# Half of the ELU gates on GpSimd in two operations, and projections that close only the gates they read

## The chip, the cores and the metric

The kernel runs on one core of a Trainium2 chip. The metric is the device time of one execution in microseconds (us); lower is better. Times are medians of several runs of the same program, and beside them stands one execution that was taken with the hardware profiler. The engines are named as in the profile: PE is TensorE's matmul, PEld its weight load, DVE is VectorE, ACT is ScalarE, POOL is GpSimd, SP is SyncE.

## What is computed

A top-32 attention is followed by a two-layer feed-forward net with an ELU between the layers. There are 8 batches, 8 heads, 576 tokens and a head size of 64; the model width is 512 and the hidden width 2048.

```python
scores = scale * np.matmul(q, k.transpose(0, 1, 3, 2))
kth = np.partition(scores, -top_k, axis=-1)[..., -top_k:-top_k + 1]
scores = np.where(scores >= kth, scores, -1000000000.0)
attn = np.exp(scores - np.max(scores, axis=-1, keepdims=True))
attn = attn / (np.sum(attn, axis=-1, keepdims=True) + 1e-09)
x = np.matmul(attn, v)            # heads side by side: 4608 x 512
h = x @ w_in                      # 4608 x 2048
g = np.where(h > 0.0, h, np.exp(np.minimum(h, 0.0)) - 1.0)
out = g @ w_out                   # 4608 x 512
```

## The kernel before

The attention is cut into 144 steps. A step is one tile of 128 queries of one batch with two heads (for the left-over 64 queries of each batch, four heads). The loop at the end of the kernel runs over the steps and, in each, writes out the work of several of them: it computes the scores of the step two ahead (`scores`: matmuls L300, copies on ACT L308), selects the 32nd largest score of the current step (`select`: on DVE alone, eight MAX8, L341 and L353, and six MATCH_REPLACE8, L346, in each step), masks and exponentiates the step before (`mask`: two tiny POOL operations, `neg` L366 and `gap` L368, and then two ACT passes, L369 and L370, for each head), normalises it (`normalise`: five tiny POOL operations L380 to L385 and two wide ones L387), transposes the step before that (`turn`: PE L406, ACT copies L407), and multiplies by V (`attend`: PE L432, ACT L459).

When all heads of a block of tokens are there, the feed-forward net of the block is put into a queue of pieces (`ffn_pieces`). A block has one, two or three slots of 128 tokens. First come 16 pieces `hidden(f)`, one for each group f of 128 hidden units: four matmuls into one of two PSUM buffers (L490), then on ACT a ReLU of the negated values into a tile n (L502), a ReLU into gT (L503) and an exponential of n (L504). What is then missing of the ELU is called the gate: gT becomes (n - 1) + gT, one SCALAR_TENSOR_TENSOR on DVE (L471). After them come four pieces `project(s, part)` for each slot s: each multiplies four groups of gT by w_out (L513) and the last of them copies the sum out (L522).

The function `feed` is called four times in each step. It counts up `place`, closes the gates that were put into a list at least two feeds ago (L604), and takes as many pieces from the queue as a plan by costs and due steps gives (`HIDDEN`, `PROJECT`). A gate is therefore not written where its exponential is, but some two feeds, half a step, later. Two other places close gates: `hidden` closes the oldest when more than three are open (L485 to L487), and `project` closes all that are open (L508). At the end a loop writes out what is left in the queue, with no feeds between.

From step 8 on the order on PE, ACT, DVE and POOL is the order in which the program is written (`manual_schedule`); in the eight steps before a scheduler may move instructions. In those first steps the weights also arrive as 64-bit floats and are decoded to 32 bits, on ACT (L169 to L171), POOL (L172, L186) and DVE (L179, L182). The first five blocks have one slot, so their gates are 128 columns wide; later gates are 256 or 384 wide. In all there are 304 gates.

Of the kernel before, what the change touches and what calls it, by code (L numbers as in the profile page):

```python
# [9 lines left out]
ALU = mybir.AluOpType  # L10
# [70 lines left out]
def kernel(  # L81
# [9 lines left out]
    nc = tc.nc  # L91
# [9 lines left out]
    NF = dff // P  # L101
# [362 lines left out]
    gates = []  # L464
    place = [0]

    def close_gates(keep=0):

        while gates and gates[0][0] <= place[0] - keep:
            _, dst, n = gates.pop(0)  # L470
            nc.vector.scalar_tensor_tensor(  # L471
                out=dst, in0=n, scalar=-1.0, in1=dst, op0=ALU.add, op1=ALU.add
            )

    def ffn_pieces(blk):
        n_tok = blk.slots * P

        def hidden(f):
            if f == 0 and blk.number == 0:
                g = early.tile([P, NF, P], FP32, tag="g", name="gT")  # L480
                blk.gT = [g[:, 0:NG], g[:, NG:NF]]
            elif f % NG == 0 and blk.number > 0:
                g = late["g"].tile([P, NG, T], FP32, tag="g", name="gT")
                blk.gT.append(g[:])
            if len(gates) > 3:  # L485
                gates[0] = (-1, *gates[0][1:])
                close_gates(place[0])  # L487
            ps = ps_f.tile([P, dm], FP32, tag="f", name="hps")
            for i in range(NC):
                nc.tensor.matmul(  # L490
                    ps[:, 0:n_tok],
                    w_in[:, i, f * P : (f + 1) * P],
                    blk.xT[:, i, 0:n_tok],
                    start=(i == 0),
                    stop=(i == NC - 1),
                )
            if blk.number == 0:
                n = earlyf.tile([P, P], FP32, tag="n", name="n")[:]
            else:
                n = late["f"].tile([P, T], FP32, tag="n", name="n")[:, 0:n_tok]  # L500
            g = blk.gT[f // NG][:, f % NG, 0:n_tok]
            nc.scalar.activation(n, ps[:, 0:n_tok], AF.Relu, scale=-1.0)  # L502
            nc.scalar.activation(g, ps[:, 0:n_tok], AF.Relu)  # L503
            nc.scalar.activation(n, n, AF.Exp, scale=-1.0)  # L504
            gates.append((place[0], g, n))

        def project(s, part):
            close_gates()  # L508
            if part == 0:
                blk.o = ps_f.tile([P, dm], FP32, tag="f", name="ops")  # L510
            step = NF // 4
            for f in range(part * step, (part + 1) * step):
                nc.tensor.matmul(  # L513
                    blk.o[:],
                    blk.gT[f // NG][:, f % NG, s * P : (s + 1) * P],
                    w_out[:, f, :],
                    start=(f == 0),
                    stop=(f == NF - 1),
                )
            if part == 3:  # L520
                o = opool.tile([P, dm], FP32, tag="osb", name="osb")
                nc.scalar.copy(o[:], blk.o[:])  # L522
                for t in blk.tiles[s]:
                    p0 = t.cols.start - s * P
                    nc.sync.dma_start(out[t.rows, :], o[p0 : p0 + t.ql, :])

        part = HIDDEN[blk.slots]
        behind = 2 * NF if blk.number else 0
        return [
            (part, max(behind, NC * (f // 4 + 1)), lambda f=f: hidden(f))  # L530
            for f in range(NF)
        ] + [
            (PROJECT, max(behind, NF + (part + 1) * NF // 4),
             lambda s=s, part=part: project(s, part))
            for s in range(blk.slots)
            for part in range(4)
        ]
# [4 lines left out]
    for b in range(B):  # L542
        if b % 2 == 0:
# [5 lines left out]
            for part in division:  # L549
                blk = Block(len(blocks), len(part))  # L550
# [20 lines left out]
        for qts in order:  # L571
            for hp in range(NHP // 2 if qts == (J,) else NHP):
                group = Group([tiles[qt] for qt in qts], hp)
                steps += [Step(tiles[qt], hp, group, i) for i, qt in enumerate(qts)]
            for qt in qts:
                n = len(steps)
# [12 lines left out]
    for b in range(1, B):  # L589
        f = first[b]  # L590
# [10 lines left out]
    def feed(n, share):  # L601

        place[0] += 1
        close_gates(2)  # L604
        fed["at"] = max(fed["at"], n)
        ahead = [(w - fed["sum"]) / (x - fed["at"]) for x, w in due if x > fed["at"]]
        if ahead:
            fed["over"] += max(0.0, share * min(ahead))
        fed["at"] += share
        while ffn and decoded[0] >= ffn[0][1] and 0.5 * ffn[0][0] <= fed["over"]:  # L610
            cost, _, piece = ffn.pop(0)
            fed["over"] -= cost
            fed["sum"] += cost
            piece()
# [115 lines left out]
```

## Time and profile before

| What | us |
|---|---|
| median of three runs (1694.2 to 1695.28) | 1694.59 |
| the profiled execution, its own time | 1695.23 |
| span of the profile, first to last instruction | 1693.4 |
| PE busy, 8560 matmuls | 1597.5 (94%) |
| DVE busy, 3248 instructions | 1542.7 (91%) |
| ACT busy | 1179.6 (70%) |
| POOL busy | 627.0 (37%) |

The profile page gives the busy time of each engine over the span, a strip of 40 slices with the busy share of each in tenths, the chain of work that ended last, and groups of instructions by line and shape. A row of a group has its count, the busy time in us, the mean of one in ns, and the idle time of the engine just before these instructions with what ended it. The trace answers further questions: busy times in chosen stretches of time, of all instructions or of one line's alone; who waited for whom; and the instructions in order of time. The ends of matmuls are modelled and matmuls overlap, so a PE that is always busy need not run at its peak.

### The profile page before, as it was taken

What the parts mean: (1) busy time and instruction counts of PE and PEld (TensorE: products, weight loads), DVE (VectorE), ACT (ScalarE), POOL (GpSimd) and SP (SyncE); (2) the same over time, 40 slices, a digit from 0 to 9 for tenths busy, and PEclk for the clock granted to TensorE, in tenths of its full rate; (3) what the DMA queues carried; (4) which work ended last, traced back from release to release, by engine and by line L of the source; (5) the groups of instructions that cost most, each with busy time, mean ns of one, the idle gap of its engine ahead of it and who ended that gap; (6) DMA issues with size and microseconds to landing.
All of it is one profiled execution on the core that took longest, in us unless ns stands there. A gap on an engine that the chain in (4) does not pass through costs nothing.

```text
span 1693.4 us, 26805 instructions
## 1 busy us (share of the span) xinstructions
PE 1597.5 (94%) x8560; PEld 1035.0 (61%) x8560; DVE 1542.7 (91%) x3248; ACT 1179.6 (70%) x2813; POOL 627.0 (37%) x1719
## 2 busy tenths in 40 slices
PE   4568899999999999999999999999999999999999
PEld 3355676667575666756557575755557575755565
DVE  6889999999999999999999999999998999998600
ACT  5787776778776776857758585867758686857531
POOL 3675333343333333433333333333333333332200
PEclk8568999999999999999999999999999999999999
DMA  5531021001200111001100111001100000000000
GB/s 156 169 130 63 15 56 36 7 1 42 51 12 7 29 35 42 1 14 42 43 19 1 28 42 35 7 10 46 36 20 8 21 21 28 7 7 7 7 13 13
DMA packets 101131, 56.25 MB, mean 33 GB/s; under 512 B 84096, under 2 KB 92288, under 8 KB 100992
## 3 DMA queue, kind: packets, MB, share of 16 engines
q1 hardware_dynamic: 100992, 54.55, 11.7%
q8 instruction: 68, 1.11, 0.3%
q14 instruction: 71, 0.58, 0.1%
HBM read 45.09 MB, written 9.44 MB: 32 GB/s over the span
## 4 chain that ended last, share of the span: by engine, by line
PE 68%; DVE 21%; ACT 5%; issue 2%; POOL 2%; DMA 1%; SPq 0%; ACTq 0%; POOLq 0%; DVEq 0%
PE ops L513 25%; PE hps L490 21%; PE avps L432 8%; DVE wk L346 7%; PE scps L300 7%; DVE m L353 6%; PE eps L406 5%; DVE m L341 2%; DVE gT L471 1%; DVE wk L323 1%; DVE m L329 1%; PE qkps L270 1%; ACT sc L370 1%; ACT sc L369 1%; ACT et L407 1%
## 5 line engine op out<-in xcount | busy, mean ns | idle before, releaser
L353 DVE MAX8 m<-wk 128x8 f32<-128x576 f32 x816 | 574.9, 745 | 0.0
L490 PE MATMUL hps<-xT,w_in 128*128 128x256 f32 (+2 forms) x2432 | 554.3, 376 | 19.3 <-ACT gT L503 19.3
L513 PE MATMUL ops<-w_out,gT 128*128 128x512 f32 x1152 | 522.6, 598 | 0.0
L490 PEld LDWEIGHTS hps<-xT,w_in 128*128 128x128 f32 x2432 | 409.5, 194 | 119.9 <-ACT gT L503 26.4
L346 DVE MATCH_REPLACE8 wk<-m,wk 128x576 f32<-128x576 f32 x544 | 399.4, 741 | 0.0
L513 PEld LDWEIGHTS ops<-w_out,gT 128*128 128x128 f32 x1152 | 208.4, 190 | 232.8 <-issue 201.0
L380 POOL TENSOR_SCALAR dene<-den 128x2 f32<-128x2 f32 x144 | 34.9, 243 | 819.6 <-ACT sc L370 819.0
L369 ACT ACTIVATE sc<-sc,neg 128x576 f32<-128x576 f32 x288 | 226.5, 787 | 56.6 <-POOL neg L366 56.1
L370 ACT ACTIVATE sc<-sc,gap 128x576 f32<-128x576 f32 x288 | 223.2, 775 | 26.6 <-ACT sc L369 1.9
L308 ACT ACTIVATE sc<-scps 128x576 f32<-128x576 f32 x288 | 173.4, 661 | 82.4 <-PE scps L300 82.4
L387 POOL TENSOR_SCALAR sc<-sc,rec 128x576 f32<-128x576 f32 x288 | 218.7, 769 | 15.2 <-POOL rec L385 0.4
L300 PE MATMUL scps<-kqT 64*128 64x288 f32 (+1 forms) x1280 | 198.1, 438 | 21.5 <-ACT sc L308 14.7
L471 DVE SCALAR_TENSOR_TENSOR gT<-n,gT 128x256 f32<-128x256 f32 (+2 forms) x304 | 129.1, 431 | 95.3 <-ACT n L504 95.3
L407 ACT COPY et<-eps 128x512 f32<-128x512 f32 x288 | 167.4, 581 | 61.8 <-PE eps L406 61.8
L406 PEld LDWEIGHTS eps<-ident,sc 128*128 128x128 f32 x1152 | 144.5, 145 | 93.4 <-issue 48.9
L346 DVE MATCH_REPLACE8 wk<-m,sc 128x576 f32<-128x576 f32 x272 | 199.7, 741 | 0.0
L432 PE MATMUL avps<-et,vT 128*64 128x256 f32 (+2 forms) x2080 | 191.0, 325 | 9.0 <-ACT et L407 8.4
L406 PE MATMUL eps<-ident,sc 128*128 128x128 f32 x1152 | 177.9, 280 | 21.8 <-POOL sc L387 18.6
L341 DVE MAX8 m<-sc 128x8 f32<-128x576 f32 x272 | 191.3, 744 | 0.0
L432 PEld LDWEIGHTS avps<-et,vT 128*64 128x64 f32 x2080 | 122.3, 140 | 80.4 <-issue 24.7
L502 ACT ACTIVATE n<-hps 128x256 f32<-128x256 f32 (+2 forms) x304 | 112.6, 370 | 84.2 <-PE hps L490 79.0
L300 PEld LDWEIGHTS scps<-kqT 64*128 64x128 f32 (+1 forms) x1280 | 106.0, 180 | 90.2 <-issue 45.1
(47 smaller groups left out, 1236.6 us busy)
## 6 DMA issues: line engine op xcount, KB each, us to landing
kin<-in_k_dram SPq DMA_DIRECT2D x64, 128.0 KB, 2.8
qin<-in_q_dram SPq DMA_DIRECT2D x64, 128.0 KB, 2.8
raw<-in_moe_w_in_dram SPq DMA_DIRECT2D x16, 512.0 KB, 3.9
vT<-in_v_dram SPq DMA_DIRECT2D x64, 128.0 KB, 2.3
raw<-in_moe_w_out_dram SPq DMA_DIRECT2D x16, 512.0 KB, 3.3
out_dram<-osb SPq DMA_DIRECT2D x32, 256.0 KB, 2.2
kin<-in_k_dram SPq DMA_DIRECT2D x32, 32.0 KB, 2.5
kin<-in_q_dram SPq DMA_DIRECT2D x32, 32.0 KB, 2.2
```

The lines of the kernel that those rows point to most:

```text
L300: nc.tensor.matmul(wide[i][rows, half, 0:HS], kq[part, q0 : q0 + u.t.ql], kq[part, k0 : k0 + HS], start=True, stop=True,)
L341: nc.vector.max(found[i], cur[i])
L346: nc.vector.match_replace(wk[i], found[i], cur[i], TAKEN)
L353: nc.vector.max(found[i], cur[i])
L369: nc.scalar.activation(sc, sc, AF.Prelu, bias=neg[:], alpha=STEEP)
L370: nc.scalar.activation(sc, sc, AF.Exp, bias=gap[:], accum_out=u.den[:, i : i + 1])
L387: nc.gpsimd.tensor_scalar(u.sc[:, i, :], u.sc[:, i, :], rec[:, i : i + 1], 1.0, ALU.mult, ALU.mult)
L406: nc.tensor.transpose(ps[:, c * P : (c + 1) * P], sc[:, c0 : c0 + P], ident[:])
L407: nc.scalar.copy(g.et[:, chunks, u.at, :], ps[:, 0 : n * P].rearrange("p (c q) -> p c q", c=n),)
L432: nc.tensor.matmul(ps[i * D : (i + 1) * D, cols], vt[:, 2 * J + i if c == J else i * J + c, :], w, start=(c == 0), stop=(c == J),)
L490: nc.tensor.matmul(ps[:, 0:n_tok], w_in[:, i, f * P : (f + 1) * P], blk.xT[:, i, 0:n_tok], start=(i == 0), stop=(i == NC - 1),)
L513: nc.tensor.matmul(blk.o[:], blk.gT[f // NG][:, f % NG, s * P : (s + 1) * P], w_out[:, f, :], start=(f == 0), stop=(f == NF - 1),)
```

## The change

Each gate is stored with its block and group. A gate of an even group stays on DVE as it was. A gate of an odd group goes to POOL, in two operations: n - 1 into n, and gT + n into gT. A projection closes the gates of its own block up to the last group that it reads, no longer all that are open. The rule in `hidden` closes the oldest gate as before, written in the new way.

```diff
-    def close_gates(keep=0):
-
-        while gates and gates[0][0] <= place[0] - keep:
-            _, dst, n = gates.pop(0)
-            nc.vector.scalar_tensor_tensor(
-                out=dst, in0=n, scalar=-1.0, in1=dst, op0=ALU.add, op1=ALU.add
-            )
+    def close_gates(keep=0, upto=None):
...
+        while gates:
+            put, group, dst, n = gates[0]
+            if put > place[0] - keep if upto is None else group > upto:
+                return
+            gates.pop(0)
+            if group[1] % 2 == 0:
+                nc.vector.scalar_tensor_tensor(
+                    out=dst, in0=n, scalar=-1.0, in1=dst, op0=ALU.add, op1=ALU.add
+                )
+            else:
+                nc.gpsimd.tensor_scalar_add(n, n, -1.0)
+                nc.gpsimd.tensor_tensor(dst, dst, n, ALU.add)
...
             if len(gates) > 3:
-                gates[0] = (-1, *gates[0][1:])
-                close_gates(place[0])
+                close_gates(upto=gates[0][1])
...
-            gates.append((place[0], g, n))
+            gates.append((place[0], (blk.number, f), g, n))
 
         def project(s, part):
-            close_gates()
+            close_gates(upto=(blk.number, (part + 1) * NF // 4 - 1))
```

Set side by side, the two built programs have the same instructions in the same order on PE, ACT and SP. DVE has 152 gates fewer (2234 instructions for 2386, as the program counts them), and 15 others, in the first steps, stand at another place. POOL has 304 operations more (2028 for 1724), and 3 others, in the first steps too, stand at another place.

## The prediction on record

> **What bounds the kernel now.** I read the page's busy strip first, then the groups by line and shape, then the busy times in chosen stretches, then the waits.
>
> ```profile
> span 1693.4 us, 26805 instructions
> PE 1597.5 (94%) x8560; PEld 1035.0 (61%) x8560; DVE 1542.7 (91%) x3248; ACT 1179.6 (70%) x2813; POOL 627.0 (37%) x1719
> PE   4568899999999999999999999999999999999999
> ...
> DVE  6889999999999999999999999999998999998600
> ```
>
> Two engines are nearly full, so neither share alone tells the bound. The stretches do:
>
> ```profile
> 100.00:200.00 100.00, 82.04 (x531) 62.76 (x527) 96.56 (x201) 78.10 (x216) 55.15 (x106) 0.88 0.20 65
> 200.00:800.00 600.00, 577.04 (x3426) 385.55 (x3426) 600.00 (x1289) 442.43 (x1093) 224.99 (x664) 1.00 0.10 27
> 800.00:1600.00 800.00, 797.34 (x4086) 499.84 (x4086) 761.92 (x1604) 569.13 (x1313) 288.14 (x840) 1.00 0.08 21
> 1600.00:1693.00 93.00, 89.42 (x308) 52.60 (x304) 6.81 (x16) 24.25 (x66) 4.09 (x12) 1.00 0.04 14
> ```
>
> The columns are stretch, length, then busy us of PE, PEld, DVE, ACT, POOL. From 200 to 800 us DVE is busy for 600.00 of 600 us and PE stands idle for 23.0: DVE is the bound. From 800 to 1600 PE is idle for 2.7 of 800 us and DVE for 38.1: PE is the bound. The rest is a feed-forward tail without DVE. DVE work taken away before 800 us can bring the end forward; taken away later it only makes DVE wait more. These are the gates and their waits:
>
> ```profile
> L471 DVE SCALAR_TENSOR_TENSOR gT<-n,gT 128x256 f32<-128x256 f32 x176 | 74.5, 424 | 86.7 <-ACT n L504 86.7
> L471 DVE SCALAR_TENSOR_TENSOR gT<-n,gT 128x128 f32<-128x128 f32 x80 | 28.1, 371 | 0.6 <-ACT n L504 0.6
> L471 DVE SCALAR_TENSOR_TENSOR gT<-n,gT 128x384 f32<-128x384 f32 x48 | 26.5, 555 | 8.1 <-ACT n L504 8.1
> ```
>
> In all they take 129.1 us. The idle time belongs to the PE-bound part and the tail: between 200 and 800 us DVE has none.
>
> **What the Trainium skill says.** "GPSIMD Engine Reference", section 3.1, gives the two-input add on GpSimd as 4497 ns for 2048 elements against 2293 ns on VectorE. The trace agrees in size: the integer add L186 of 512 columns takes 1275 to 1316 ns. "SBUF — State Buffer", in "SBUF: two separate sides", says that a VectorE operation with two SBUF inputs and a GpSimd operation that reads SBUF take an exclusive lock, and the later one waits for the whole of the other. The trace shows it in part: DVE gates have a median of 407 ns over all shapes and a worst case of 1233, while the MAX8 row (one input) has a mean of 745 and hardly spreads, though POOL runs beside it for 37% of the span. "Perfetto Trace Analysis", under the GPSIMD instruction, warns that GpSimd spans are unreliable and to be read from start to start; here the timeline at 913 us has chained POOL operations of 190 to 200 ns that start 280 to 290 ns apart, so I add 0.09 us for each such link.
>
> **The change part by part.**
>
> DVE loses 152 of 304 gates, half of each shape: 129.1 / 2 = 64.6 us. By stretch, with the busy time of line L471 alone (rounded), its half, and PE's idle time:
>
> | us | gates | half | PE idle | smaller |
> |---|---|---|---|---|
> | 200-300 | 8.0 | 4.0 | 7.6 | 4.0 |
> | 300-400 | 7.7 | 3.9 | 5.6 | 3.9 |
> | 400-500 | 7.9 | 3.9 | 2.4 | 2.4 |
> | 500-600 | 8.8 | 4.4 | 3.6 | 3.6 |
> | 600-700 | 7.1 | 3.5 | 0.7 | 0.7 |
> | 700-800 | 8.3 | 4.2 | 3.1 | 3.1 |
>
> A stretch gets shorter by the DVE time it loses until PE has no idle time left, so the smaller of the two counts: 17.7 of 23.9 us.
>
> POOL gains the two operations. One-input: 209 ns for 2 columns (L384) and a median of 612 for 512 (L172) give 0.79 ns per column, 0.41 us for 256. Two-input: 204 ns for 2 columns (L383) and about 1290 for 512 give 2.1 ns per column, 0.74 us for 256. With the link that is 1.24 us; the same for 128 columns gives 0.87 and for 384 gives 1.61. The sum is 88 x 1.24 + 40 x 0.87 + 24 x 1.61 = 183 us, and POOL goes from 627 to some 810 us, 48%. It has room. It isn't the sum that can hurt but the order.
>
> The lock: in a step with gates, about 10.9 us long, POOL's two two-input adds cover 1.5 us, 14%; a DVE gate that meets one waits about half of it, 0.37 us. For the 63 DVE gates left before 800 us that is 3 us. Where DVE's relief exceeds PE's idle time it costs nothing, so I take 1; bounds 0 and 63 x 0.37 = 23.
>
> From 100 to 200 us half of 13.2 us, 6.6, goes from DVE too, and PE has 18 us idle there. But POOL also decodes weights: DVE's L179 waits 25.2 us in all for POOL's L172, and nine POOL gates of 0.87 us, 7.8 us, now stand in that queue. I take half of it as reaching DVE: a gain of 2.5; bounds -4 and +6.6.
>
> Behind a POOL gate stand, on POOL, the negation L366 of the mask, for which ACT's L369 waits, and then everything behind it on ACT: PSUM evacuations, transposed copies, and so PE. By the program's order 64 POOL gates stand between a normalisation and the next L366, 35 of them in the PE-bound part. In a PE-bound step with gates the negation ends at 915.35 us and ACT's L369 starts at 915.87:
>
> ```profile
> 913.51 1.63 POOL L387 TENSOR_SCALAR sc<-sc,rec 128x576 f32<-128x576 f32 x2
> ...
> 915.12 0.23 POOL L366 TENSOR_SCALAR neg<-m 128x1 f32<-128x1 f32 x1
> ...
> 915.87 0.78 ACT L369 ACTIVATE sc<-sc,neg 128x576 f32<-128x576 f32 x1
> ```
>
> A gate of 1.24 us there makes ACT 0.7 us late. ACT is idle for 29% of this part, and in the list of waits PE waits for it only 2.2 us from 800 to 1600 us, so most is absorbed: I take 35 x 0.1 = 3.5 us; bounds 0 and 35 x 0.7 = 24.5. Before 800 us the same delay shifts ACT by a step's fraction while DVE sets the pace; nothing. The other things behind a POOL gate, gap, the second head's negation and the normalisation, wait for ACT's L370 anyway (819 us of idle time before L380).
>
> The projection's narrower closing removes DVE waits for exponentials just written. From 800 to 1600 us DVE waits 32.4 us for L504, all under a PE that is 99.7% busy: worth nothing, and before 800 there is no such wait. It also lets the last odd gate come late; a projection reads group 15 only 12 matmuls of 0.43 us, 5.2 us, after its start, which covers 1.24. If that cover were gone, each block would pay at most 1.24 us. The closing rule in `hidden` is the same as before. SP's order and all DMAs stay.
>
> Sum: 17.7 - 1 + 2.5 - 3.5 + 0.5 (the idle time of PE after 800 us that DVE might end) = 16.2 us. Profiled execution 1695.23 - 16.2 = 1679.0; the median of the runs lies 0.64 below that execution, so 1678.4. I predict 1678.
>
> **The rivals.**
>
> A. PE's idle time isn't DVE's doing. From 75 to 500 us the list of waits has PE waiting 19.3 us (8.1 and 11.2) for ACT's L503 in the 128-column blocks; if ACT is the limit there, DVE's relief turns into DVE idle time. For it: these waits; against it: DVE has no idle time from 200 us on while ACT is busy for 442 of 600 us, 74%. Left are the gains after 500 us, 7.4, less 3.5: 1691.
>
> B. Slower: the POOL gate before the negation. In the PE-bound half each of 35 gates makes ACT 0.7 us late and PE as late, 24.5 us; the lock takes 10 of the 20 us gained. 1694.6 + 24.5 - 10 = 1709. It decides from a PE loss of about 0.6 us per gate on. For it: negation directly behind the normalisation, ACT in order; against it: the 2.2 us above, so there is some slack between ACT and PE.
>
> C. More: matmul ends are modelled, so PE's real idle time is larger than its busy share tells, and relief left over in one stretch is used in the next. Then 23.9 + 6.6 + 0.5 = 31: 1664.
>
> D. The change doesn't do what it says: excluded as to where gates go, by the program's order.
>
> **How the numbers follow.** Forecast 0.60 at 1678, A 0.14, B 0.13, C 0.13. 0.2% is 3.4 us, about what a measurement of this kernel can tell from no change. The forecast, C and a little of A are faster: 0.75; A's rest and the edge of B the same: 0.13; B slower: 0.12. Range 1664 to 1695: it takes in C and A and leaves out B and some 0.05 below.
>
> **What would show it.** Right: DVE busy near 1480 us, POOL near 810, PE's idle time from 200 to 800 us down to a few us, DVE idle time appearing before 800 us, the MAX8 rows unchanged. Wrong: PE idle over 5 us between 800 and 1600 us with ACT's L369 waiting longer on L366 (56.1 us now) means B; DVE idle before 500 us with PE's idle time unchanged means A; DVE gates over 500 ns on average mean the lock.

## The result, and the profile after

The changed kernel takes 1716.37 us (median of four runs, 1715.2 to 1718.14), the kernel before, run beside it, 1694.93 (1694.2 to 1695.52): a ratio of 1.0128, 95% interval 1.011 to 1.0145, slower by 21.4 us. The profiled execution took 1715.67 us, with a span of 1713.9. That is the side of rival B, and beyond the time that B named.

The head of the page after the change, with the strips of PE and DVE:

```profile
span 1713.9 us, 26892 instructions
...
PE 1604.6 (94%) x8560; PEld 1034.4 (60%) x8560; DVE 1494.4 (87%) x3096; ACT 1179.2 (69%) x2813; POOL 854.5 (50%) x2023
...
PE   4568999989999999999999999999999999999999
DVE  6878999999999999998999989898997989897600
```

DVE is 48.3 us less busy, where 64.6 were expected, and POOL 227.5 us more, where 183 were expected. PE does the same work in a longer span. The same stretches as before, with busy us of PE, PEld, DVE, ACT and POOL, say where it got worse:

```profile
100.00:200.00 100.00, 79.48 (x494) 60.85 (x491) 86.71 (x179) 73.67 (x201) 67.01 (x128) 0.86 0.20 65
200.00:800.00 600.00, 572.76 (x3412) 381.97 (x3412) 579.75 (x1222) 438.36 (x1087) 302.94 (x780) 1.00 0.10 26
800.00:1600.00 800.00, 791.94 (x4071) 495.38 (x4070) 733.63 (x1524) 565.95 (x1310) 402.26 (x968) 1.00 0.08 21
```

DVE now has 20 us of idle time between 200 and 800 us, and still PE is idle there for 27.2 us where it was 23.0; between 800 and 1600 it is idle for 8.1 us where it was 2.7. The relief arrived at DVE, and PE came out later all the same. What PE waits for more are results of ACT. These are the largest such waits of the changed kernel, each before and then after (total, times, longest, in us), first from 200 to 800 us, then from 800 to 1600:

```profile
PE hps L490 <- ACT gT L503: 11.2, 14, 1.6
PE hps L498 <- ACT gT L511: 16.1, 19, 1.9
...
PE avps L432 <- ACT et L407: 0.2, 1, 0.2
PE avps L432 <- ACT et L407: 4.1, 7, 1.6
```

The groups with the gates and with the mask's wait (count, then busy us, mean ns, idle time before and what ended it). The first line is of the kernel before, the others of the changed one:

```profile
L369 ACT ACTIVATE sc<-sc,neg 128x576 f32<-128x576 f32 x288 | 226.5, 787 | 56.6 <-POOL neg L366 56.1
...
L369 ACT ACTIVATE sc<-sc,neg 128x576 f32<-128x576 f32 x288 | 226.5, 787 | 103.9 <-POOL neg L366 103.6
...
L481 POOL TENSOR_SCALAR n<-n 128x256 f32<-128x256 f32 x88 | 77.1, 876 | 39.4 <-ACT n L512 39.4
L482 POOL TENSOR_TENSOR gT<-gT,n 128x256 f32<-128x256 f32 x88 | 65.1, 740 | 7.3
...
L477 DVE SCALAR_TENSOR_TENSOR gT<-n,gT 128x256 f32<-128x256 f32 x88 | 40.8, 464 | 121.9 <-ACT n L512 121.7
L353 DVE MAX8 m<-wk 128x8 f32<-128x576 f32 x816 | 574.0, 743 | 0.0
```

Three things are to be seen. The two-input half of a POOL gate takes 740 ns, for which 737 were expected. The one-input half takes 876, for which 410 were expected. And the wait of ACT for the negation has grown from 56.1 to 103.6 us. Here is one such place in the order of time, the same step of the program that the prediction showed (start, duration, engine):

```profile
925.69 1.48 POOL L387 TENSOR_SCALAR sc<-sc,rec 128x576 f32<-128x576 f32 x2
...
927.14 0.87 POOL L481 TENSOR_SCALAR n<-n 128x256 f32<-128x256 f32 x1
...
928.10 0.73 POOL L482 TENSOR_TENSOR gT<-gT,n 128x256 f32<-128x256 f32 x1
...
928.80 0.23 POOL L366 TENSOR_SCALAR neg<-m 128x1 f32<-128x1 f32 x1
...
929.07 0.77 ACT L369 ACTIVATE sc<-sc,neg 128x576 f32<-128x576 f32 x1 [1.24 <-POOL neg L366]
```

From the start of the normalisation to that of ACT's mask it was 2.36 us before (913.51 to 915.87); now it is 3.38. The pair stands in between with 1.66 us from its first start to the start of the negation, and ACT has stood idle for 1.24 us.

The order of the instructions on PE is the same in both kernels, so each matmul can be looked up in both traces, and the difference of its starts tells how late PE is by then. I call this PE's shift. For the changed kernel it is +4.9 us at 200 us of the kernel before, +12.1 at 800 and +20.4 at the end. So the loss comes in three parts: 4.9 before 200 us, 7.2 between 200 and 800, 8.3 after that.

The shift compares two single executions, and their granted clocks differ in places. In the trace of the kernel before, the clock drops from 727 to 731 us (the third number from the end of the line; on both sides of it, it is 1.00):

```profile
727.00:731.00 4.00, 3.81 (x18) 2.05 (x18) 4.00 (x11) 1.23 (x3) 2.77 (x6) 0.57 0.00 0
```

All kernels below whose trace has no such drop there gain 1.7 us against it, whatever their edit, so this part of a shift says nothing of an edit. From 100 to 200 us the mean clock of the traces lies between 0.83 and 0.91, and two kernels with the same POOL gates, the changed one and the one with all open gates closed at a projection, have +4.9 and +6.7 at 200 us. A shift there is good to some 2 us.

### The profile page after: what moved, and what is told of

It reads as the page before. It is cut to its first block, busy times and chain, and to the rows that moved or that the text cites. A ratio compares the mean times of both kernels' runs of the same rounds, so it can differ in the third digit from the quotient of the medians.

```text
span 1713.9 us, 26892 instructions
## 1 busy us (share of the span) xinstructions
PE 1604.6 (94%) x8560; PEld 1034.4 (60%) x8560; DVE 1494.4 (87%) x3096; ACT 1179.2 (69%) x2813; POOL 854.5 (50%) x2023
## 3 DMA queue, kind: packets, MB, share of 16 engines
q1 hardware_dynamic: 100992, 54.55, 11.6%
## 4 chain that ended last, share of the span: by engine, by line
PE 64%; ACT 13%; DVE 9%; POOL 8%; issue 4%; DMA 1%; SPq 0%; ACTq 0%; POOLq 0%
PE ops L521 27%; PE hps L498 16%; PE avps L432 8%; PE scps L300 6%; PE eps L406 4%; ACT sc L369 4%; ACT sc L370 3%; DVE wk L346 3%; DVE m L353 2%; ACT et L407 2%; POOL sc L387 2%; POOL n L481 1%; ACT n L510 1%; ACT n L512 1%; POOL gT L482 1%
## 5 line engine op out<-in xcount | busy, mean ns | idle before, releaser
L380 POOL TENSOR_SCALAR dene<-den 128x2 f32<-128x2 f32 x144 | 33.8, 235 | 646.6 <-ACT sc L370 646.1
L369 ACT ACTIVATE sc<-sc,neg 128x576 f32<-128x576 f32 x288 | 226.5, 787 | 103.9 <-POOL neg L366 103.6
L308 ACT ACTIVATE sc<-scps 128x576 f32<-128x576 f32 x288 | 173.4, 662 | 77.6 <-PE scps L300 77.5
L387 POOL TENSOR_SCALAR sc<-sc,rec 128x576 f32<-128x576 f32 x288 | 214.7, 756 | 15.0
L300 PE MATMUL scps<-kqT 64*128 64x288 f32 (+1 forms) x1280 | 196.5, 436 | 19.5 <-ACT sc L308 15.7
L407 ACT COPY et<-eps 128x512 f32<-128x512 f32 x288 | 167.4, 581 | 52.6 <-PE eps L406 52.5
L477 DVE SCALAR_TENSOR_TENSOR gT<-n,gT 128x256 f32<-128x256 f32 (+2 forms) x152 | 67.9, 447 | 153.0 <-ACT n L512 152.8
L341 DVE MAX8 m<-sc 128x8 f32<-128x576 f32 x272 | 190.5, 740 | 0.0
L300 PEld LDWEIGHTS scps<-kqT 64*128 64x128 f32 (+1 forms) x1280 | 105.5, 179 | 87.1 <-issue 45.3
```

What stands on the lines that cost most here:

```text
L300: nc.tensor.matmul(wide[i][rows, half, 0:HS], kq[part, q0 : q0 + u.t.ql], kq[part, k0 : k0 + HS], start=True, stop=True,)
L341: nc.vector.max(found[i], cur[i])
L369: nc.scalar.activation(sc, sc, AF.Prelu, bias=neg[:], alpha=STEEP)
L387: nc.gpsimd.tensor_scalar(u.sc[:, i, :], u.sc[:, i, :], rec[:, i : i + 1], 1.0, ALU.mult, ALU.mult)
L407: nc.scalar.copy(g.et[:, chunks, u.at, :], ps[:, 0 : n * P].rearrange("p (c q) -> p c q", c=n),)
```

## The experiments

Each kernel was timed beside the kernel before. A ratio below is of the experiment to the kernel before, with its 95% interval. The kernel before took 1692.1 to 1695.4 us in these series, so it is differences and ratios that can be compared between them, not times.

### Only the narrower closing, and only the gates on GpSimd

The change has two parts. The first kernel keeps every gate on DVE:

```diff
-            if group[1] % 2 == 0:
+            if True:
```

> All gates stay on DVE; only the narrower closing at projections is kept. Main theory (the POOL gates stand in front of the masks' negations and make ACT and then PE late): about the time before, 1695 us, within 3. Rival (the narrower closing reorders DVE and costs by itself): 1700 to 1716.

Measured: 1694.6 us, ratio 0.9995 (0.9987 to 1.0004). The second kernel keeps the odd gates on POOL, but a projection closes all that are open:

```diff
-            close_gates(upto=(blk.number, (part + 1) * NF // 4 - 1))
+            close_gates()
```

> Odd gates on POOL as in the changed kernel; a projection again closes all open gates. Main theory: as the changed kernel, 1716 us, within 5. Rival (the closing costs): clearly below, 1695 to 1705.

Measured: 1717.55 us, ratio 1.0126 (1.0111 to 1.0141), the same as the whole change. All of the loss is in the gates on POOL. The narrower closing costs and brings nothing.

### Relief alone: the odd gates left out

```diff
             else:
-                nc.gpsimd.tensor_scalar_add(n, n, -1.0)
-                nc.gpsimd.tensor_tensor(dst, dst, n, ALU.add)
+                pass
```

> The odd gates are left out altogether, so half of the hidden units lack the exponential part: DVE gets the relief and POOL gets nothing. If DVE's relief is worth what the prediction says: 1673 to 1679 us. If PE is not paced by DVE from 200 to 800 us: 1691 to 1696.

Measured: 1688.04 us, ratio 0.9951 (0.9935 to 0.9968): 7.4 us less than the kernel before (5 to 11 by the interval), between the two expectations and nearer to the second. DVE has all the relief of the change here, and nothing pays for it. So the relief is worth 7.4 us, less than half of the 17.7 and 2.5 in my sum, and everything that POOL does to the changed kernel costs 7.4 + 21.4 = 28.8 us.

PE's shift shows where the 7.4 us come from: it is +0.9 at 500 us, -1.2 at 550, -1.2 at 700, -4.6 at 750 and -5.3 at the end. (It need not give the medians' 7.4.) Of the fall from 700 to 750 us, 1.7 are the drop of the clock in the trace of the kernel before. PE gains at two places, 1.77 us at each of two single matmuls (at 539.7 and 725.1 us of the kernel before), and up to 500 us not at all. At the first of them the kernel before has this chain (in brackets the idle time of the engine, and what ended it):

```profile
536.98 0.23 POOL L366 TENSOR_SCALAR neg<-m 128x1 f32<-128x1 f32 x1 [2.80 <-DVE m L353]
...
537.25 0.78 ACT L369 ACTIVATE sc<-sc,neg 128x576 f32<-128x576 f32 x1 [3.04 <-POOL neg L366]
...
539.67 1.23 PE L300 MATMUL scps<-kqT 64*128 64x288 f32 x6 [1.39 <-ACT et L407]
```

POOL waits for DVE's last maximum, ACT for POOL's negation, and PE for the copy that ACT makes after the mask. There DVE does set the pace. The changed kernel has the same two gains of 1.77 us; they are only outweighed.

### More relief: all gates left out

Is DVE's relief too small, or is it of no use?

```diff
             if group[1] % 2 == 0:
-                nc.vector.scalar_tensor_tensor(
-                    out=dst, in0=n, scalar=-1.0, in1=dst, op0=ALU.add, op1=ALU.add
-                )
+                pass
             else:
-                nc.gpsimd.tensor_scalar_add(n, n, -1.0)
-                nc.gpsimd.tensor_tensor(dst, dst, n, ALU.add)
+                pass
```

> All 304 gates are left out, so every hidden unit lacks the exponential part: DVE loses 129 us and POOL gets nothing. Leaving out half of them was worth 7 us. If DVE's pace limits PE (the prediction's reading of a DVE that is never idle): twice that or more, 15 to 23 us below the kernel before. If PE is paced by its round trips with ACT: 7 to 11 us below.

Measured: 1686.97 us, ratio 0.9954 (0.9939 to 0.9968), 7.8 us less than the kernel before. Twice the relief gives the same gain. The head of its page, and the same stretches:

```profile
PE 1597.6 (95%) x8560; PEld 1035.4 (61%) x8560; DVE 1441.3 (85%) x2944; ACT 1178.2 (70%) x2813; POOL 605.5 (36%) x1719
```

```profile
200.00:800.00 600.00, 579.93 (x3436) 388.21 (x3432) 581.68 (x1202) 445.37 (x1099) 216.39 (x662) 1.00 0.11 27
800.00:1600.00 800.00, 797.37 (x4080) 498.30 (x4079) 690.66 (x1420) 564.42 (x1303) 275.88 (x843) 1.00 0.08 21
```

DVE does 101.4 us less in all. What becomes of it is in the waits of its DVE (total, times, longest, in us):

```profile
DVE m L341 <- ACT sc L308: 88.6, 61, 8.1
```

DVE runs ahead: from the 36th of the 144 steps on it begins a step 18 to 32 us earlier than in the kernel before, until it reaches scores that ACT has not yet copied. In the kernel before there is no such wait between 200 and 800 us. There the scores of a step are ready about 20 us before DVE reads them (copies L308 against the first MAX8 L341 of the same tile). DVE was full without being late: it worked off a stock of ready scores, and what it made was not needed at once, except at the two places above. PE still has 20.1 us of idle time between 200 and 800, so most of that was never DVE's. Its largest wait there is for ACT's ReLU, as before, when it was 11.2 us:

```profile
PE hps L495 <- ACT gT L508: 11.1, 14, 1.6
```

The next two waits for ACT stay as well, 5.7 us for L308 (5.8 before) and 2.4 for L407 (2.4 before). What has gone is the 2.8 us of the two matmuls L300 at 539.7 and 725.1 us.

### POOL's occupation alone

The reverse of it: the kernel before, with all gates on DVE, and the pair added on POOL on a tile of its own. It waits for no exponential, and nobody needs it. From step 8 on the pair stands at the places of the odd gates. In the first steps, where the scheduler may move instructions, the eight pairs of the first block run from 2 to 15 us, while the changed kernel has these gates from 113 to 162 us, and the order on PE differs too, up to some 140 us. So this kernel and the next one can speak only for what comes after the decode stage.

```diff
+    idle = const.tile([P, T], FP32, tag="idle", name="idle")
+    nc.gpsimd.memset(idle[:], 0.0)
...
-            if group[1] % 2 == 0:
-                nc.vector.scalar_tensor_tensor(
-                    out=dst, in0=n, scalar=-1.0, in1=dst, op0=ALU.add, op1=ALU.add
+            nc.vector.scalar_tensor_tensor(
+                out=dst, in0=n, scalar=-1.0, in1=dst, op0=ALU.add, op1=ALU.add
+            )
+            if group[1] % 2 == 1:
+                w = dst.shape[-1]
+                nc.gpsimd.tensor_scalar_add(idle[:, 0:w], idle[:, 0:w], -1.0)
+                nc.gpsimd.tensor_tensor(
+                    idle[:, 0:w], idle[:, 0:w], idle[:, 0:w], ALU.subtract
                 )
-            else:
-                nc.gpsimd.tensor_scalar_add(n, n, -1.0)
-                nc.gpsimd.tensor_tensor(dst, dst, n, ALU.add)
```

> The kernel before, all gates on DVE, with the changed kernel's pair of POOL operations added at the places of the odd gates, on a small tile of their own that waits for no exponential. If POOL's occupation ahead of the negations and of the decode is the whole cost: the cost that the changed kernel has over the one with the odd gates left out, 28 us, so 1717 to 1723 with the kernel before at 1693. If waits for exponentials, or the gates' late results, count: below 1710.

Measured: 1717.57 us, ratio 1.0133 (1.0116 to 1.015), 22.8 us more than the kernel before. ACT's wait for the negation is nearly that of the changed kernel:

```profile
ACT sc L371 <- POOL neg L368: 98.7, 62, 5.4
```

From 200 us to the end PE's shift grows by 16.1 us, in the changed kernel by 15.5. So from there on POOL's being occupied at these places makes most of the loss, without any dependence between the gates and the rest. Left, if the first steps cost the same in both (PE is 6.4 us late by 200 us here, 4.9 in the changed kernel), is 28.8 - 22.8 = 6 us. For that the two were put together: the odd gates left out, and the free pair in their places.

```diff
             else:
-                nc.gpsimd.tensor_scalar_add(n, n, -1.0)
-                nc.gpsimd.tensor_tensor(dst, dst, n, ALU.add)
+                w = dst.shape[-1]
+                nc.gpsimd.tensor_scalar_add(idle[:, 0:w], idle[:, 0:w], -1.0)
+                nc.gpsimd.tensor_tensor(
+                    idle[:, 0:w], idle[:, 0:w], idle[:, 0:w], ALU.subtract
+                )
```

> The changed kernel with the odd gates left out and, in their places, the same two GpSimd operations on a tile of their own: DVE has its relief, POOL its occupation, but POOL waits for no exponential and no projection waits for POOL. (Half of the hidden units lack the exponential part.) It splits what is open between the pair added to the kernel before (22.8 us for the occupation alone) and the changed kernel with its odd gates left out (28.9 us for everything on POOL). If the 6 us are POOL waiting for exponentials, and projections waiting for the late gates: 1694.8 - 7.4 + 22.8 = 1710. If they are not, and the relief of DVE is simply worth nothing once ACT and PE are late: 1716 to 1717, as the changed kernel. I lean to 1710, since the trace of the changed kernel has POOL standing idle 39.4 us ahead of the first operation of the 256-column pairs for an exponential.

Measured: 1713.11 us, ratio 1.0118 (1.0101 to 1.0135), 19.3 us more than the kernel before. It lies between the two expectations, and its interval overlaps that of the changed kernel. By medians some 3.5 of the 7.4 us of relief are left beside the occupation (22.8 to 19.3), and some 2 us come from POOL's waiting for exponentials or from late gates (19.3 to 21.4). Each of these is below what the intervals can tell apart. The traces place a part of it: the two gains of 1.77 us at 539.7 and 725.1 us are in the kernel with the pair only added too. Just before the first of them PE is 13.9 us late there and DVE only some 6 to 8, so the wait has gone without any relief. The 22.8 us are thus net of 3.5 us that the relief can't bring a second time. How the other 2.5 us divide stays open.

### The negation ahead of the POOL gates

If the gates hurt because of what stands behind them, it must help to put that ahead of them. The negation and the gap of both heads are written right after the normalisation, ahead of the step's last feed; no operation is added.

```diff
+    def negate(u, i):
+
+        if i in u.ready:
+            return
+        low, top = u.last[:, i, 7:8], u.first[:, i, 0:1]
+        neg = small.tile([P, 1], FP32, tag="neg", name="neg")
+        nc.gpsimd.tensor_scalar_mul(neg[:], low, -1.0)
+        gap = small.tile([P, 1], FP32, tag="gap", name="gap")
+        nc.gpsimd.tensor_tensor(gap[:], low, top, ALU.subtract)
+        u.ready[i] = neg, gap
+
...
-        neg = small.tile([P, 1], FP32, tag="neg", name="neg")
-        nc.gpsimd.tensor_scalar_mul(neg[:], low, -1.0)
-        gap = small.tile([P, 1], FP32, tag="gap", name="gap")
-        nc.gpsimd.tensor_tensor(gap[:], low, top, ALU.subtract)
+        negate(u, i)
+        neg, gap = u.ready[i]
...
+        if cur:
+            for i in range(2):
+                negate(cur, i)
```

> The changed kernel with the negation and gap of both heads written at the end of a step, right behind the normalisation and ahead of the fourth feed, so that from step 8 on no gate stands between a normalisation and the next negation. Theory (the gates ahead of the negation make ACT's L369 and so PE late): the loss after 350 us shrinks, 1716 to 1700-1706, and L369's wait falls from 104 us to below 60. Rival (POOL's occupation delays the normalisation, or waits for exponentials count): over 1712.

Measured: 1694.2 us beside 1692.07, ratio 1.0013 (1.0006 to 1.002). Of 21.4 us, 2.1 are left, fewer than the theory had expected. The mask's wait and the stretches:

```profile
L379 ACT ACTIVATE sc<-sc,neg 128x576 f32<-128x576 f32 x288 | 226.7, 787 | 44.5 <-POOL neg L364 44.4
```

```profile
200.00:800.00 600.00, 579.65 (x3474) 389.10 (x3472) 588.48 (x1239) 445.91 (x1109) 308.60 (x795) 1.00 0.10 27
800.00:1600.00 800.00, 797.36 (x4086) 499.00 (x4086) 738.86 (x1534) 569.17 (x1314) 400.66 (x978) 1.00 0.08 21
```

POOL is as busy as in the changed kernel, and PE's idle time from 800 to 1600 us is back at 2.6. The wait for the negation is 44.4 us. PE's shift is +6 from 200 to 500 us, then falls with DVE's relief, and by the 1.7 us of the drop of the clock, to +0.7 at 750 and ends at +0.2. The edit also brings the second head's negation ahead of gates, but in the changed kernel ACT's wait for a negation after 200 us, 83.5 us in all, is always at a step's first head. So the gates that count are those between a normalisation and the next negation. Does the early negation help by itself? The control is the kernel before with the same edit:

> Control: the kernel before with the same early negations, all gates on DVE. If the place of the negation matters only with gates in front of it: 1695 us, within 2. If the negation was late already: 1688 to 1692.

Measured: 1692.32 us, ratio 1.0004 (0.9995 to 1.0012). It does nothing there, so what it gives back is what the gates cost through the negation: 21.4 - 2.1 = some 19 us.

### The one-input half with two scalars

POOL's rows of before that do one multiplication and one addition in an instruction (L384) are quick for their size, quicker than the row that adds one scalar to the same two columns (L380):

```profile
L380 POOL TENSOR_SCALAR dene<-den 128x2 f32<-128x2 f32 x144 | 34.9, 243 | 819.6 <-ACT sc L370 819.0
...
L384 POOL TENSOR_SCALAR dene<-dene 128x2 f32<-128x2 f32 x144 | 30.1, 209 | 12.6
```

The same n - 1, written with a multiplication by 1:

```diff
-                nc.gpsimd.tensor_scalar_add(n, n, -1.0)
+                nc.gpsimd.tensor_scalar(n, n, 1.0, -1.0, ALU.mult, ALU.add)
```

> The changed kernel with the one-input POOL operation written with two scalars (n x 1 - 1), as the kernel's other POOL operations are. In the profile of the changed kernel it takes 873 ns for 256 columns against the 410 that I had worked out from L384 and L172. If the form is what makes it slow: about 410 ns now. Main theory: the loss goes with the length of the gate, 1.68 to 1.24 us, so the time falls from 1716 to some 1705 to 1710. Rival (the loss lies in waiting for exponentials, not in the gate's length): 1714 to 1717.

Measured: 1703.76 us, ratio 1.0045 (1.003 to 1.006), 8.3 us more than the kernel before and some 13 less than the changed one. The groups of this kernel:

```profile
L369 ACT ACTIVATE sc<-sc,neg 128x576 f32<-128x576 f32 x288 | 226.5, 787 | 81.3 <-POOL neg L366 81.0
...
L481 POOL TENSOR_SCALAR n<-n 128x256 f32<-128x256 f32 x88 | 36.1, 410 | 43.7 <-ACT n L512 43.7
```

The form that does twice the arithmetic takes less than half the time, 410 ns for 876. A POOL gate shorter by 0.47 us gives back 13 us: the loss goes with the length of the gate, as a queue ahead of something urgent would have it.

### The decode stage: the first block's gates on DVE

```diff
-            if group[1] % 2 == 0:
+            if group[1] % 2 == 0 or group[0] == 0:
```

> The changed kernel, but the gates of block 0, which fall into the steps in which POOL decodes weights, stay on DVE. In the changed kernel PE is 5 us late by 150 us. If POOL's gates in the decode cause that: 1711 us, and PE's lateness at 200 us gone. Rival (the decode has slack, the lateness comes from the list order): 1715 to 1717.

Measured: 1711.08 us beside 1692.07, ratio 1.0113 (1.0098 to 1.0128). PE's shift at 200 us falls from 4.9 to 1.8, and 1.9 us of it are left at the end (18.5 for 20.4). The intervals of the two ratios overlap, so the end alone would not show it, and at 200 us a shift is good to some 2 us. At 150 us, where the kernels with these gates on POOL in the same form agree better (4.5 to 5.1), it falls from 5.1 to 0.9. The waits from 100 to 200 us say why. They have this line in the kernel before, in the changed one and in this one:

```profile
DVE raw L179 <- POOL raw L172: 2.9, 3, 1.4
DVE raw L179 <- POOL raw L172: 12.1, 9, 3.2
DVE raw L179 <- POOL raw L172: 2.9, 3, 1.5
```

In the changed kernel these eight gates make DVE's decode wait for POOL's, and cost some 3 us in the decode stage.

### Does the exponential hold PE up before 500 us?

What PE waits for there was to be found by leaving ACT's exponential out in the one-slot blocks of the kernel before:

```diff
-            nc.scalar.activation(n, n, AF.Exp, scale=-1.0)
+            if blk.slots > 1:
+                nc.scalar.activation(n, n, AF.Exp, scale=-1.0)
```

> The kernel before without the exponential of the gates in the five blocks of one slot (the ELU's negative part is wrong there): ACT loses 80 x 0.315 = 25 us before 400 us, DVE keeps its gates. If PE's idle time before 500 us is ACT's round trip: PE is 5 to 12 us early by 500 us. If DVE sets the pace: less than 2 us.

Measured: 1698.14 us, ratio 1.0022 (1.0014 to 1.0029): slower with less work. This doesn't answer the question. The edit also changed how the scheduler ordered the first steps (the order on PE differs up to 145 us), and DVE is some 4 us late from the tenth step on. PE is 3.0 us late at 500 us and 2.5 at the end.

### All three mends together

The gates on POOL with two scalars, those of the first block on DVE, and the early negation:

```diff
-            if group[1] % 2 == 0:
+            if group[1] % 2 == 0 or group[0] == 0:
...
-                nc.gpsimd.tensor_scalar_add(n, n, -1.0)
+                nc.gpsimd.tensor_scalar(n, n, 1.0, -1.0, ALU.mult, ALU.add)
...
+        if cur:
+            for i in range(2):
+                negate(cur, i)
```

> The changed kernel with two scalars, block 0 on DVE and early negations together. If the three costs are all: about the time with the odd gates left out, 1688 us, and at most 1692. If POOL costs something besides: 1695 to 1700.

Measured: 1688.25 us beside 1692.07, ratio 0.9977 (0.9968 to 0.9986): 3.8 us less than the kernel before, and so faster than both. The 1688 of the expectation is met, but the kernel before was quicker in this series, so the gain is half of that of the kernel with the odd gates left out (0.9951). The two intervals meet at 0.9968: whether POOL costs something besides can't be told. PE's shift is -0.2 at 500 us, -5.8 at 800 and -6.4 at the end. In it are the two gains of the relief and the 1.7 us of the drop of the clock in the trace of the kernel before.

```profile
200.00:800.00 600.00, 580.00 (x3453) 388.08 (x3453) 587.66 (x1239) 446.94 (x1106) 282.82 (x790) 1.00 0.11 27
800.00:1600.00 800.00, 797.36 (x4085) 497.91 (x4082) 731.97 (x1523) 564.88 (x1304) 363.01 (x978) 1.00 0.08 21
```

## Why the prediction was wrong

It forecast 1678 and the time is 1716.4, 38 us more. The difference splits by two measured sums: the relief is 7.4 us and not the 20.7 that I had summed (17.7, 2.5 and 0.5), and POOL costs 28.8 us and not 4.5 (3.5 and 1). That is 13.3 and 24.3 us, together 37.6.

By stretch, PE's shift puts it so, each number to within some 2 us (relief: the kernel with the odd gates left out; POOL: the changed kernel less that one):

| stretch, us | relief | POOL | together |
|---|---|---|---|
| up to 200 | -0.8 | +5.7 | +4.9 |
| 200 to 800 | -3.8 | +11.0 | +7.2 |
| 800 to the end | -0.7 | +9.0 | +8.3 |

The steps of the prediction:

- "DVE is busy for 600.00 of 600 us and PE stands idle for 23.0: DVE is the bound." This failed. Of PE's 23.0 us of idle time, 20.1 are still there when all 304 gates are gone. The table that took the smaller of relief and idle time supposed that PE's idle time is DVE's doing in each stretch. That was rival A, whose reasons held: up to 500 us PE gains nothing, and its wait for ACT's ReLU stays at 11.1 us. That A's 7.4 us of gain after 500 are also the 7.4 measured is luck: A summed PE's idle time, of which 2.8 us went away. What speaks against A in my text, that DVE has no idle time, says nothing about who is waited for, since an engine with 20 us of ready work in front of it is never idle.
- "64.6 us" for DVE: the page's DVE fell by 48.3. A gate's row also counts a time in which the next instruction has begun (in the changed kernel a gate runs from 920.42 to 920.82 us and the next instruction starts at 920.75): 0.076 us on average, 11.6 us for 152 gates, that were never DVE's to lose. Another 3.3 us are the gates that stayed, which grew from 425 to 447 ns. It decided nothing.
- "0.41 us for 256", the one-input half of a POOL gate: mis-sized, 876 ns. Both rows that I took the price from, L384 and L172, have two scalars and two operations in one instruction. L380, which adds one scalar to the same 2 columns, takes 243 ns where L384 takes 209, and that was on record in the trace of the kernel before; I read it as the same kind. So a gate is some 1.7 us instead of 1.24, and POOL is busy for 854.5 us instead of 810. This is worth some 13 us.
- "A gate of 1.24 us there makes ACT 0.7 us late", "35 x 0.1 = 3.5 us", and before 800 us "nothing": the mechanism was named, the size and the place were wrong. By the early negation it is worth some 19 us. Over the 64 gates that stand there in the whole kernel that is 0.3 us each (the 13 us above are in part the same loss, since a shorter gate makes a shorter queue, so the two don't add up). And 11.0 us of POOL's cost come between 200 and 800 us, where I had put nothing because DVE "sets the pace". PE waited only 2.2 us for ACT from 800 to 1600 us before, and I took that for slack. It wasn't slack: a small wait tells that two chains are nearly equal as well as that one is far ahead.
- In the decode stage, "a gain of 2.5": the sign was wrong. PE is 4.9 us late by 200 us; some 3 of that belong to the eight POOL gates of the first block. The bound of -4 was too near.
- The lock: right in size. In the changed kernel a DVE gate of 256 columns takes 411 ns with no POOL operation beside it (22 cases). Of those that start while POOL's two-input half runs, the 12 that find more than 0.15 us of it left all end 0.28 us after it does, and take 651 ns on average and 902 at most; the MAX8 row stays at 743. So a gate waits for the rest of the operation. This is the exclusive lock that the Trainium skill states in "SBUF — State Buffer", section "SBUF: two separate sides". I had reckoned with the two-input half alone, but the one-input normalisation L387 holds gates up in the same way, in the kernel before too (gates of up to 887 ns), so a part of it was there already. Few gates meet it: the mean over all DVE gates is 447 ns, 22 more than before and under the 500 that I had named as a sign.
- The narrower closing at nothing: right (0.9995). The tail without DVE: right, PE's shift there is constant.

Rival B had the mechanism, with 24.5 us in the PE-bound half, less 10. That it came within 8 us is in part luck: after 800 us POOL costs 9.0 us, 0.26 for each of the 35 gates and not 0.7, and what B left out before 800 us made up for it. Its sign decided: PE's idle time of 8.1 us from 800 to 1600, with ACT's wait for the negation at 103.6 us.

Two things stay open: how the last 2.5 us divide between relief that is lost beside the occupation and waits of the gates, and why ACT is late for PE in the 20 us of idle time before 800 us that are not DVE's. The experiment on the exponential did not answer that.

## What to carry to other kernels

An engine that is never idle is the bound only if somebody waits for what it makes: look at how long its inputs have been ready and its outputs lie unread, and, if in doubt, leave its work out and time that. Before work goes to an engine with room, find the short operations on it that others wait for, and count what would stand ahead of each; here 227 us more on a half-idle queue cost 29 us, and writing the two tiny operations of each head earlier gave back 19. "Perfetto Trace Analysis", section "Optimizing Scalar/DVE Operations", of the Trainium skill holds that offloading to GpSimd may make sense when DVE is saturated, and also that it might not help; here it did only with those operations out of the way, the gates written in the shorter form and those of the first block on DVE, and then for 3.8 us.

## What was not expected of the hardware

On GpSimd a TENSOR_SCALAR that adds one scalar is slower than one that multiplies by a scalar and adds another: 551, 876 and 1252 ns for 128, 256 and 384 columns, against 307, 410 and 569. From 128 to 384 columns the first grows by 2.7 ns a column, the second by 1.0. "GPSIMD Engine Reference", section 4.1, of the Trainium skill has one-input operations as roughly line-rate. Of these two forms only the second is near to VectorE, whose gate, where no POOL operation runs beside it, takes 274, 410 and 540 ns in the kernel before: 1.0 ns a column too.
